# RWKV-6 attention feeding a gated MLP: the first chunk's softplus, Erf and multiplication of the sixth step take another place

## The chip, the cores and the metric

The kernel runs on one core of a Trainium2 chip. The metric is the device time of one execution in microseconds (us). The kernel before was timed three times: 603.26, 604.39 and 604.74 us, median 604.39 us.

The engines are named as in the profile: PE does matrix products (PEld loads their weights), DVE elementwise work and reductions, ACT activations and copies, POOL elementwise work too, and SP issues DMA transfers. Each engine works through its own queue of instructions in order; engines wait for each other by semaphores.

## The reference

Two blocks follow each other. The first is an attention with a decaying state, the second a projection, a gate, and a projection back:

```python
# r, k, v, w: (batch 4, heads 8, sequence 768, head_dim 48); u: (8, 48)
for t in range(S):
    cur = einsum('bhd,bhe->bhde', u * k[t], v[t])
    y[t] = einsum('bhd,bhde->bhe', r[t], state + cur)
    state = w[t][..., None] * state + einsum('bhd,bhe->bhde', k[t], v[t])

x = y as (3072 tokens, 384)
h = x @ w_in                                   # 384 -> 2048
sp = maximum(h, 0) + log1p(exp(-abs(h)))       # softplus
out = (h * erf(sp)) @ w_out                    # 2048 -> 384
```

All of it is in float32.

## The kernel before

**Steps.** The sequence is cut into 6 blocks of 128 tokens and the batch into 2 pairs, which gives 12 steps (s = 0 to 11) of 256 tokens each. In step s the attention of step s is computed while the hidden layer of step s-1 (function `hidden`, line 777: x @ w_in into a PSUM tile m, then a copy to h by ACT at line 786) and the projection back of step s-3 (function `project`, line 809, up to step 2, `project_fast`, line 885, from step 3 on) are spread between its parts. Step 5 is the sixth, and the first that runs through `attend_late`.

**The order is written by hand.** Within the scheduled region the instructions stand in each engine's queue in the order in which the Python code issues them. For the late steps a table of strings, `LATE` (with `USUAL` for the steps that have no row of their own), says what is issued at seven places of a step, named by `STAGES_LATE`: "front", "near", 0, 1, 2, 3, 4. `run_late` reads the string of the place, token by token:

- `s`: the softplus of the next chunk (line 733, ACT), into one SBUF buffer, `sp_room`, which all chunks share
- `ey`, `ep`: its Erf (line 737, ACT), from `sp_room` into a PSUM tile: y, or the lane pp1. Ahead of each softplus and each Erf ACT loads a table
- `m`: the multiplication h = h * Erf (line 742, DVE), reading the tile of the oldest Erf still open
- `P`, `H`: a piece of the projection back or of the hidden layer (PE, with ACT's copy of a finished tile)
- `F`: the next part of what is prepared for step s+1 (function `prepare`)
- `k22y`, `k11p`, `k12y`: a copy of a quarter of h into y or pp1 (line 845, ACT)
- `S1` to `S4`: sums and differences of quarters on DVE (lines 862 to 868)

A chunk is a quarter of a step's hidden layer, 128 x 1024 elements. The chunks of step 3's hidden layer are worked off in step 5.

**The places around the change, in `attend_late`.** At the start of the step come the products of a level (line 452, PE), a scaling (line 263, DVE) and a masked copy (line 464, DVE). Then follows the place "front". The first two parts of `prepare(s + 1)` follow: on POOL the running products of the decay (line 315), on DVE the near products: one product with u (line 384) and, for distances 1 to 4, the terms (line 377) and the new k (line 381). Then follows the place "near". The next part sums the terms 1 to 3 (line 367, DVE), gives POOL the terms 5 to 8, makes one product (line 398, DVE), sums the terms 0 and 4 and gives POOL the terms from 9 on; POOL's term 5 goes into the buffer that the sums read. Then DVE multiplies kT by the spread decay (line 597), the place 0 follows, then the last level's products (line 452), the spreading of blocks (line 551, copied by ACT at line 557), ACT's copies at line 471 and a scaling on DVE, then the place 1, the state products (line 538, PE), and the places 2 to 4.

**Buffers that couple the engines.** The PSUM tile y is the target of every `ey` and of `k22y` and `k12y`; an Erf into it waits until the multiplication that read its last content is done. The two PSUM tiles m of the pool `ps_m` hold the projection's outputs in step 5 until ACT has copied them (line 818); the hidden layer's pieces (line 777) then take turns in the same two tiles.

Of the kernel before, what the change touches and what calls it, by code (L numbers as in the profile page):

```python
# [17 lines left out]
P = 128  # L18
# [43 lines left out]
def kernel(  # L62
# [881 lines left out]
    def in_order(s, k):  # L944
# [3 lines left out]
        for what in order[k]:  # L948
# [8 lines left out]
    STAGES_LATE = ("front", "near", 0, 1, 2, 3, 4)  # L957
    LATE = {
        DIRECT + 1: (
            "", "", "s ey m P s ep m P P s P ey m P", "s P F ep m P k22y F P k11p F", "S1",  # L960
            "S2 S3 H k12y S4 H F", "s H ep m H H F G s H H H ep",
        ),
        n_steps - 1: (
# [57 lines left out]
    with tc.manual_schedule(  # L1021
# [72 lines left out]
        s = n_steps  # L1094
# [104 lines left out]
```

## Time and profile before

The profiled execution took 603.48 us; its span, from the first to the last instruction, is 601.5 us. Its mean granted TensorE clock is 0.997 of full speed.

| engine | busy us | share of the span |
|---|---|---|
| PE | 585.6 | 97% |
| PEld | 501.7 | 83% |
| DVE | 439.9 | 73% |
| ACT | 362.0 | 60% |
| POOL | 272.3 | 45% |

The part of the sixth step around the change, as the timeline of the trace has it:

| instruction | start us | duration us |
|---|---|---|
| ACT: first chunk's softplus (L733) | 207.97 | 1.06 |
| ACT: first chunk's Erf into y (L737) | 210.34 | 1.03 |
| DVE: last near product (L381) | 213.30 | 0.76 |
| DVE: sums of terms 1 to 3 (L367) | 213.97 | 2.37 |
| POOL: first term (L377) | 214.95 | 1.31 |
| DVE: product L398 | 216.25 | 0.95 |
| DVE: sums of terms 0 and 4 (L367) | 217.24 | 1.61 |
| DVE: product into kT (L597) | 218.77 | 1.72 |
| DVE: first chunk's multiplication (L742) | 220.41 | 1.21 |
| DVE: second chunk's multiplication (L742) | 221.54 | 1.21 |
| ACT: third chunk's Erf into y (L737) | 222.99 | 1.03 |
| DVE: third chunk's multiplication (L742) | 224.05 | 1.22 |
| ACT: fourth chunk's Erf into pp1 (L737) | 229.42 | 1.03 |
| DVE: fourth chunk's multiplication (L742) | 230.48 | 1.22 |

The table shows when each instruction began and how long it took; an engine's queue is in this order, so what stands above on the same engine is done first. Consecutive instructions on DVE overlap by some 0.1 us in the records.

### The profile page before, as it was taken

The page shows a single profiled execution, that of the slowest core. Times are in us where ns is not written, and L with a number is a line of the kernel's source. Part 1 is how long each engine was busy: PE and PEld are TensorE (multiplying, and loading weights), DVE is VectorE, ACT ScalarE, POOL GpSimd, SP SyncE. Part 2 cuts the span into 40 slices and gives each one's busy share as a digit, 9 for nine tenths or more (in the row PEclk, how much of TensorE's full clock was granted, in tenths as well). Part 3 has the DMA queues.
Part 4 walks back from the last instruction along what each step waited for, and adds up shares of the span by engine and source line. Part 5 has one row for each costly group of instructions (what it writes and reads, how often), then busy time and mean ns, then how long its engine had stood idle before and what let it go on. Part 6 is the DMA issues. An engine that isn't in the chain of part 4 may idle for free.

```text
span 601.5 us, 16645 instructions
## 1 busy us (share of the span) xinstructions
PE 585.6 (97%) x7290; PEld 501.7 (83%) x7290; DVE 439.9 (73%) x516; ACT 362.0 (60%) x473; POOL 272.3 (45%) x296
## 2 busy tenths in 40 slices
PE   7889999999999997999999999999999999999997
PEld 6668787578668756899899899898898898898997
DVE  5688598798996898699799799799799624124140
ACT  2548888726534477684865864765765764756710
POOL 4349275601487569429639639539549100000000
PEclk9999999999999998999999999999999999999999
DMA  8377371541314415234334324334321300000000
GB/s 323 116 278 231 131 273 61 212 142 20 140 50 155 93 48 192 46 105 169 71 105 168 71 105 169 72 106 133 71 106 54 71 9 26 2 21 13 2 27 26
DMA packets 51376, 63.33 MB, mean 105 GB/s; under 512 B 34920, under 2 KB 40296, under 8 KB 49896
## 3 DMA queue, kind: packets, MB, share of 16 engines
q1 hardware_dynamic: 50824, 62.03, 31.9%
q8 instruction: 57, 0.93, 0.6%
q10 hardware_dynamic: 480, 0.25, 0.2%
q14 instruction: 15, 0.12, 0.1%
HBM read 52.39 MB, written 8.69 MB: 102 GB/s over the span
## 4 chain that ended last, share of the span: by engine, by line
PE 81%; DVE 8%; DMA 4%; ACT 3%; issue 2%; POOL 2%; SPq 0%; POOLq 0%; DVEq 0%; ACTq 0%
PE m L777 38%; PE m L885 28%; PE m L809 4%; PE pp L452 4%; DMA w<-in_rkw 3%; PE y L486 2%; PE y L512 1%; DVE in L263 1%; PE pp L538 1%; DVE sums L367 1%; DVE words L381 1%; DVE rk L377 1%; POOL tot_sb L315 1%; POOL w_in_sb L232 1%; DVE own L464 1%
## 5 line engine op out<-in xcount | busy, mean ns | idle before, releaser
L777 PE MATMUL m<-xT,w_in_sb 128*128 128x256 f32 x1152 | 259.3, 383 | 5.7 <-ACT o L818 3.2
L777 PEld LDWEIGHTS m<-xT,w_in_sb 128*128 128x128 f32 x1152 | 217.2, 191 | 38.9 <-issue 3.8
L786 ACT COPY h<-m 128x512 f32<-128x512 f32 x96 | 55.8, 582 | 85.8 <-PE m L777 85.7
L263 DVE TENSOR_TENSOR in<-in,tot_sb 128x1024 f32<-128x1024 f32 (+1 forms) x60 | 78.7, 1311 | 24.6 <-PE pp L452 21.6
L377 POOL TENSOR_TENSOR rk<-words 128x528 f32<-128x528 f32 (+3 forms) x28 | 40.7, 1455 | 98.5 <-DVE sums L367 88.1
L381 POOL TENSOR_TENSOR words<-words,rest 128x528 f32<-128x528 f32 (+10 forms) x77 | 79.5, 1033 | 6.0
L809 PE MATMUL m<-w_out_sb,h 128*128 128x384 f32 x192 | 64.3, 491 | 0.0
L809 PEld LDWEIGHTS m<-w_out_sb,h 128*128 128x128 f32 x192 | 35.7, 190 | 23.6
L885 PE MATMUL m<-mixed,h 128*128 128x192 f32 x288 | 51.1, 331 | 0.0
L885 PE MATMUL m<-w_out_sb,h 128*128 128x192 f32 x288 | 50.3, 329 | 0.0
L737 ACT ACT_TABLE_LOAD x36 | 46.2, 1283 | 4.9 <-DVE h L742 3.2
L733 ACT ACT_TABLE_LOAD x36 | 46.2, 1283 | 2.6 <-issue 2.0
L885 PEld LDWEIGHTS m<-w_out_sb,h 128*128 128x128 f32 x288 | 46.9, 190 | 0.5
L885 PEld LDWEIGHTS m<-mixed,h 128*128 128x128 f32 x288 | 46.6, 190 | 0.9
L452 PEld LDWEIGHTS pp<-in 48*64 48x64 f32 (+1 forms) x2368 | 33.8, 125 | 14.4 <-issue 7.7
L885 PE MATMUL m<-w_out_sb,room 128*128 128x192 f32 x256 | 44.2, 326 | 0.0
L315 POOL TENSOR_TENSOR tot_sb<-tot_sb 128x256 f32<-128x256 f32 (+4 forms) x60 | 40.4, 673 | 4.5
L742 DVE TENSOR_TENSOR h<-h,y 128x1024 f32<-128x1024 f32 x17 | 20.7, 1215 | 29.6 <-ACT y L737 29.5
L885 PEld LDWEIGHTS m<-w_out_sb,room 128*128 128x128 f32 x256 | 42.0, 190 | 0.0
L452 PE MATMUL pp<-in 48*64 48x64 f32 (+1 forms) x2368 | 38.4, 212 | 3.8 <-issue 1.6
L733 ACT ACTIVATE room<-h 128x1024 f32<-128x1024 f32 x36 | 38.1, 1057 | 0.4
L742 DVE TENSOR_TENSOR h<-h,pp 128x1024 f32<-128x1024 f32 x19 | 23.0, 1212 | 20.8 <-ACT pp L737 20.8
(123 smaller groups left out, 822.1 us busy)
## 6 DMA issues: line engine op xcount, KB each, us to landing
in<-in_rkw SPq DMA_DIRECT2D x11, 1024.0 KB, 5.6
words<-in_moe_w_in SPq DMA_DIRECT2D x8, 768.0 KB, 6.2
words<-in_moe_w_out SPq DMA_DIRECT2D x8, 768.0 KB, 4.6
words<-in_rk_rows SPq DMA_DIRECT2D x8, 768.0 KB, 6.0
w<-in_rkw SPq DMA_DIRECT2D x11, 512.0 KB, 6.9
v<-in_v SPq DMA_DIRECT2D x12, 384.0 KB, 5.6
out<-o SPq DMA_DIRECT2D x24, 192.0 KB, 2.5
rest<-in_w_rows SPq DMA_DIRECT2D x8, 384.0 KB, 5.3
```

The source lines that it names most:

```text
L263: nc.vector.tensor_mul(halves, halves, view(tots[level - 1], 0, [[1, n], [2, nb], [0, half]]))
L315: nc.gpsimd.tensor_mul(new, pair[:, :, 0], pair[:, :, 1])
L377: engine.tensor_mul(terms[n], r[:, :, n:], k[:, :, : near - n])
L381: engine.tensor_mul(k[:, :, :m], k[:, :, :m], w[:, :, n : n + m])
L452: nc.tensor.matmul(pp[s0 : s0 + m, e, n, :m], lhsT=rk[rows(e), 1, n, s0 : s0 + m], rhs=rk[rows(e), 0, n, t0 : t0 + m], start=True, stop=True,)
L733: nc.scalar.activation(sp_room, chunks[0], AF.Softplus)
L737: nc.scalar.activation(at, sp_room, AF.Erf)
L742: nc.vector.tensor_mul(h, h, at)
L777: nc.tensor.matmul(ps[:, ff, :], lhsT=w_in_sb[:, g * FG + f + ff, kk * P : (kk + 1) * P], rhs=xT[:, kk, :], start=kk == 0, stop=kk == KT - 1,)
L786: nc.scalar.copy(h[:, f : f + FT, :], ps[:])
L809: nc.tensor.matmul(ps[j][:], lhsT=gs[g][:, f, j * C : (j + 1) * C], rhs=w_out_sb[:, g * FG + f, :], start=g + f == 0, stop=g == NG - 1 and ...
L885: nc.tensor.matmul(to, lhsT=a[:, f], rhs=b[:, f], start=start and f == 0, stop=f == FG - 1, skip_group_check=True,)
```

## The change

In the row of the sixth step the first chunk's softplus and Erf are issued at the place "front" instead of at the place 0, and its multiplication at the place "near". In the place 0 the remaining two chunks and the five pieces of the projection are strung in another order, and in the place 1 one piece of the projection is issued behind `k22y` instead of ahead of it. The number of each kind of token stays.

```diff
     STAGES_LATE = ("front", "near", 0, 1, 2, 3, 4)
     LATE = {
         DIRECT + 1: (
-            "", "", "s ey m P s ep m P P s P ey m P", "s P F ep m P k22y F P k11p F", "S1",
+            "s ey", "m", "s ep m P P s ey m P P P", "s P F ep m k22y P F P k11p F", "S1",
             "S2 S3 H k12y S4 H F", "s H ep m H H F G s H H H ep",
         ),
```

## The prediction

> **What bounds the kernel now.** I read the page's busy times first (PE 585.6 of 601.5 us, next DVE with 439.9), so only time in which PE stands still, or runs slowly, can be won. Then the waits between 204 and 254 us, which is the sixth step up to its last projection, PE's rows alone:
>
> ```profile
> engine line waited for: us in total, times, longest us
> PE m L777 <- ACT o L818: 3.2, 2, 2.2
> ```
>
> PE waits twice, each time for a copy of a finished output out of PSUM by ACT. PE's timeline from 226 us puts the two waits, and its granted clock by windows tells what followed (columns: us, length, then busy time and count for PE, PEld, DVE, ACT, POOL, then PEclk):
>
> ```profile
> 226.26 0.94 PE L538 MATMUL pp<-v,kT 64*48 64x48 f32 x64
> 228.16 2.86 PE L777 MATMUL m<-xT,w_in_sb 128*128 128x256 f32 x12 [0.97 <-ACT o L818]
> 233.22 20.08 PE L777 MATMUL m<-xT,w_in_sb 128*128 128x256 f32 x84 [2.20 <-ACT o L818]
> ```
> ```profile
> 231.10:233.20 2.10, 0.00 (x0) 0.00 (x0) 2.00 (x3) 1.46 (x3) 2.02 (x2) 1.00 0.00 0
> 233.20:236.00 2.80, 2.79 (x7) 2.26 (x8) 2.80 (x3) 1.76 (x3) 2.56 (x4) 0.53 0.63 202
> 236.00:239.00 3.00, 3.00 (x14) 2.56 (x13) 2.95 (x5) 1.84 (x3) 2.61 (x7) 0.87 1.00 382
> ```
>
> The reader is to see two losses: 0.97 + 2.20 = 3.17 us of standing still, and, right behind the second, a stretch at a granted clock of 0.53 and then 0.87. Its cost: the same 96 matmuls of the next step take 20.99 us (0.2186 each), so the 84 here should take 18.37 and took 20.08: 1.71 us more. Last, the chain of waits, followed back from that second wait:
>
> ```profile
> 220.49 1.14 DVE h L742
> ...
> 221.69 0.08 ACT L737
> 221.78 1.21 issue
> 222.99 1.03 ACT y L737
> ...
> 225.25 1.28 ACT L733
> ...
> 226.55 1.06 ACT room L733
> ...
> 227.63 0.48 ACT o L818
> ...
> 228.13 1.28 ACT L737
> ...
> 229.42 1.04 ACT pp L737
> ...
> 230.48 1.23 DVE h L742
> ```
>
> It goes on with the copy at L845 (231.74) and the second copy of an output (232.76 to 233.17), for which PE waits. Its root is the first chunk's multiplication on DVE at 220.41. The chunk's Erf had been ready on ACT since 210.34 + 1.03 = 211.37; but the multiplication stands behind all near products, the sums of terms 1 to 4 and the product into kT. The third chunk's Erf writes the same PSUM tile (y) and so waits for that multiplication: ACT stands still for 3.25 us (218.45 to 221.69).
>
> **What the skill says.** "TensorE: Matmul & The Clock Gate", Part 1: The HAM clock gate, states that the array falls to half of its clock after an idle window and regains it after about 3.4 us of work. The trace agrees: 0.53 of the clock after the 2.2 us gap; 1.71 us lost at half speed is 3.4 us of it. "ScalarE: Activation LUTs", What ACT_TABLE_LOAD costs: about 1283 ns for each load, whatever the set; here 1.28 us before each softplus and each Erf. "SBUF — State Buffer", Who interferes with whom: a DVE operation with two inputs in SBUF contends with GpSimd's reads. The trace agrees: the same L263 of 512 elements takes 1.43 us in this step and 0.68 in the next. The multiplication of this change has one input in PSUM.
>
> **The change part by part.** The instructions that each engine issues, and their order on PE, ACT, POOL and SP (its DMAs among them), stay as they were: nothing on these engines stands between the places from which and to which the first softplus, its Erf and one piece of the projection move. Only DVE's order changes: the first chunk's multiplication (h<-h,y) passes seven instructions: three sums, the product L398, two sums, the product into kT L597. So there is one moved operation of 1.21 us (1.14 in sequence), nothing added or removed.
>
> Its new place: DVE ends its last near product at 213.30 + 0.76 = 214.06; the Erf is done since 211.37, so it doesn't wait (2.7 us in hand). It runs 214.0 to 215.2.
>
> Behind it on DVE, seven instructions come 1.13 us later (220.41 to 221.54 is the pitch of two such multiplications): the sums start at 215.1 instead of 213.97, the product into kT ends at about 221.6 instead of 220.49. Who waits for them: POOL, whose first term follows the first sum (214.95, now 216.1), and PE's state products L538 at 226.26, which need kT: 4.6 us in hand. Cost on the path: nothing; if that cover were gone, up to 1.13 us.
>
> What it frees on ACT: the third Erf's table load starts at 218.47 instead of 221.69, 3.22 us earlier. After it ACT has no wait of its own: PE's level products end at about 218.15 and its block spreading at 218.39, before the copies L557 and L471 (now about 220.7 to 222.0); the fourth softplus ends at 224.4; the first output (8 of its 24 rows of L809 behind 218.32, so 221.0) is copied 224.4 to 224.9; the fourth Erf ends at 227.23.
>
> DVE meanwhile: multiplications two and three at 221.54 and 222.68 (the third Erf ends at 220.8, so the old idle 1.30 goes), L263 of 512 elements (pitch 1.35) from 223.8, L263 of 1024 (1.93) from 225.17 to 227.1. The fourth multiplication starts at 227.26, 3.22 us earlier. Then L845 at 228.5, the second copy of an output ends at 229.94 instead of 233.16.
>
> PE: L538 ends at about 227.2, the first copy is done at 224.9, so L777's first 12 rows start at 227.19 (0.97 gained) and end at 229.98; the second buffer is free at 229.94. The second wait is 0 to 0.05 us: all 3.17 us go. With no gap of over 0.1 us left here I see nothing to drop the clock: another 1.71. Sum 4.88 us.
>
> What is late next: L777's further pieces need their buffer emptied by ACT. At the full clock a piece takes 12 x 0.2186 = 2.62 us. The third needs a copy that ends at about 231.4, before 232.6; the fourth one at about 234.0, before 235.25; the closest is the fifth (236.9 before 237.9). PE reaches from_own at 248.35 instead of 253.23. DVE must then have L263 of the next step ready (246.31 + 1.84 = 248.15 before). It is held by the sums of POOL's terms: POOL, 1.13 us later, gives its last products at about 239.2; the sums end at about 241 instead of 244.03, and L263 at about 245, against 248.85, when PE asks for it. The DMA of the sums goes out 3 us earlier with them. From 253 us to the end the waits list none for PE, and its work there is one row behind the other, so the gain is carried to the end.
>
> The sum against the profiled execution: its own time is 603.48 (span 601.5 and 1.98 around it); less 4.88 is 598.6. The median of the runs shown is 604.39, 0.9 above; I take 604.39 - 4.88 = 599.5.
>
> Bounds of what the trace doesn't show: the clock's fall may still come elsewhere (0 to 1.71 us kept; I take 0, because the only gap left is under 0.1 us). The moved DVE work meets other POOL work: between the sums and the fourth multiplication are the product into kT (1.72 us, with 0.95 as an undisturbed size of 768 elements), and L263 at 1.43 and 1.93. They can lose or gain some 0.7 us each, since 0.68 is seen; only 0.16 us is in hand there, so a longer one shows in PE's second wait. I take 0, bounds 0 to 1.5; a gain is excluded by ACT's Erf, which ends last.
>
> **Rivals.**
> *The waits go, the clock's spell stays or comes later:* for it speaks that two gaps preceded it and the trace doesn't tell which of them counted; against it, that with both gone nothing is left to set it off, and that the lone gap of 0.99 us ahead of 69.35 us left the clock at 1.00. 604.39 - 3.17 = 601.2.
> *The second wait stays in part*, because DVE is held by POOL in kT and L263 and the fourth multiplication comes up to 1.5 us late: 599.5 + 0.7 to 599.5 + 1.5, about 600.6.
> *Swallowed later:* POOL's terms and the sums that wait for them hold DVE until PE asks for the next level product. It decides if POOL ends about 4 us later than I reckon; with that the early time is waited off: 603.5 to 604.4. Against it: POOL's 23.5 us of terms take as long in the next step (266.44 to 290), where the multiplication already stands before the sums.
> *Slower:* the first multiplication, now ahead of the sums, stands waiting for its Erf, and everything behind it on DVE (the sums, POOL's 22 operations, kT, the fourth multiplication) stands too. ACT's start there hangs on its three DMA issues (to 206.64). The path is late from 0.16 us of stall on and the gain is gone at 4.9 us, if the Erf ended at 218.9 instead of 211.37; with 7 us, 604.39 + 2.1 = 606.5. Since ACT's order didn't change, I see no reason for this delay.
>
> **How the numbers follow.** Chances: forecast (599.5, own range 598.3 to 600.3) 0.62; spell stays (601.2) 0.13; second wait in part (600.6) 0.11; swallowed 0.08; slower 0.06. The range 598.2 to 602.0 holds the first three but for a little. A measurement of this kernel tells about 0.3%, 1.8 us, from no change: all of the first three (0.86) are faster than 602.6; same 0.08; slower 0.06.
>
> **What would show it.** Right: on DVE h<-h,y directly before the three sums without idle time; ACT's wait of 3.2 us for DVE gone; PE's waits for o L818 gone; L777's 96 rows in about 21 us and a clock of 1.00 between 226 and 250 us. Wrong: DVE idle before that multiplication, a clock under 1 in this stage, a wait of PE for L263, or a DVE still busy with POOL's sums when from_own has begun.

## The result, and the profile after

The changed kernel took 598.26 us in the median of 6 executions (597.87 to 599.63), beside it the kernel before 603.83 us (601.60 to 605.25, 6 executions). The ratio is 0.9913 with a 95% interval of 0.989 to 0.9936. In a later comparison it was 598.21 us against 603.25 us, 0.9929 (0.9905 to 0.9953). The profiled execution took 598.50 us, its span is 596.3 us (before 601.5).

PE's timeline in the sixth step, as in the prediction (start, duration, instruction; idle time ahead of it would stand in brackets):

```profile
226.26 0.94 PE L538 MATMUL pp<-v,kT 64*48 64x48 f32 x64
227.12 21.01 PE L777 MATMUL m<-xT,w_in_sb 128*128 128x256 f32 x96
248.06 0.66 PE L486 MATMUL y<-own,v 64*48 64x64 f32 x32
```

L538 starts at the same 226.26 us as before. Behind it all 96 rows of L777 (records: each of these 48 float32 matmuls has two) run in one piece, without the waits of 0.97 and 2.20 us, and the products of the function `from_own` (L486), which come next, start at 248.06 instead of 253.23. The stage from L538 to from_own has shrunk from 26.97 to 21.80 us, by 5.17; the span by 5.2. From from_own to the end it is some 348.2 us in both. So the whole difference lies in this stage, and nothing of it is given back.

The windows of the changed kernel over that stretch (columns as in the prediction; the last but two is the granted clock):

```profile
228.20:231.00 2.80, 2.80 (x15) 2.36 (x14) 2.70 (x3) 2.74 (x4) 2.64 (x3) 1.00 0.18 60
231.00:234.00 3.00, 3.00 (x16) 2.64 (x15) 2.95 (x5) 1.57 (x3) 2.76 (x4) 1.00 0.91 311
234.00:237.00 3.00, 3.00 (x16) 2.64 (x15) 3.00 (x4) 2.95 (x5) 2.69 (x5) 1.00 0.70 272
```

The clock stays at 1.00 where it stood at 0.53 and 0.87. DVE's timeline of the changed kernel shows the moved instruction and what it pushes:

```profile
213.97 1.22 DVE L742 TENSOR_TENSOR h<-h,y 128x1024 f32<-128x1024 f32 x1
215.10 2.37 DVE L367 TENSOR_REDUCE sums<-rk 128x15 f32<-128x720 f32 x3
...
219.90 1.72 DVE L597 TENSOR_TENSOR kT<-kT,spread 128x768 f32<-128x768 f32 x1
221.54 1.21 DVE L742 TENSOR_TENSOR h<-h,pp 128x1024 f32<-128x1024 f32 x1
222.67 1.21 DVE L742 TENSOR_TENSOR h<-h,y 128x1024 f32<-128x1024 f32 x1
223.80 0.68 DVE L263 TENSOR_TENSOR in<-in,tot_sb 128x512 f32<-128x512 f32 x1
224.40 2.12 DVE L263 TENSOR_TENSOR in<-in,w 128x1024 f32<-128x1024 f32 x1
227.00 1.22 DVE L742 TENSOR_TENSOR h<-h,pp 128x1024 f32<-128x1024 f32 x1 [0.48 <-ACT pp L737]
...
243.21 1.68 DVE L263 TENSOR_TENSOR in<-in,tot_sb 128x1024 f32<-128x1024 f32 x1
```

The first multiplication has no idle time ahead of it, the product into kT is 1.13 us later, the fourth multiplication 3.48 us earlier, and the scaling for the next step's products (243.21 + 1.68 = 244.89) is 3.7 us ahead of PE's L452 at 248.55. ACT's timeline has the link between them. First the table load ahead of the third Erf in the kernel before, then ACT in the changed kernel:

```profile
221.69 1.28 ACT L737 ACT_TABLE_LOAD   x1 [3.25 <-DVE h L742]
```
```profile
217.14 1.06 ACT L733 ACTIVATE room<-h 128x1024 f32<-128x1024 f32 x1
218.21 1.28 ACT L737 ACT_TABLE_LOAD   x1
219.51 1.03 ACT L737 ACTIVATE y<-room 128x1024 f32<-128x1024 f32 x1
...
224.15 0.48 ACT L818 COPY o<-m 128x384 f32<-128x384 f32 x1
...
229.21 0.47 ACT L818 COPY o<-m 128x384 f32<-128x384 f32 x1
```

The third Erf's table load follows the softplus at once, where ACT waited 3.25 us before. The copies of the two outputs, for which PE used to wait, end at 224.63 and 229.68 instead of 228.11 and 233.16.

### The profile page after: what moved, and what is told of

It is laid out like the page before. It is cut to its first block, busy times and chain, and to the rows that moved or that the text cites. A ratio compares the mean times of both kernels' runs of the same rounds, so it can differ in the third digit from the quotient of the medians.

```text
span 596.3 us, 16645 instructions
## 1 busy us (share of the span) xinstructions
PE 584.7 (98%) x7290; PEld 501.7 (84%) x7290; DVE 440.1 (74%) x516; ACT 361.8 (61%) x473; POOL 274.5 (46%) x296
## 4 chain that ended last, share of the span: by engine, by line
PE 88%; DVE 6%; issue 2%; ACT 2%; DMA 1%; POOL 1%; SPq 0%; DVEq 0%; ACTq 0%; POOLq 0%
PE m L777 40%; PE m L885 28%; PE m L809 8%; PE pp L452 6%; PE y L486 2%; DVE in L263 2%; PE pp L538 1%; PE y L512 1%; DMA in<-in_rkw 1%; PE pp L680 1%; DVE sums L367 1%; DVE words L381 1%; DVE own L464 1%; ACT rk L292 1%; DVE w_in_sb L228 0%
## 5 line engine op out<-in xcount | busy, mean ns | idle before, releaser
L777 PE MATMUL m<-xT,w_in_sb 128*128 128x256 f32 x1152 | 257.3, 382 | 2.3 <-DVE w_in_sb L228 1.3
L777 PEld LDWEIGHTS m<-xT,w_in_sb 128*128 128x128 f32 x1152 | 216.0, 190 | 34.5 <-issue 3.7
L263 DVE TENSOR_TENSOR in<-in,tot_sb 128x1024 f32<-128x1024 f32 (+1 forms) x60 | 78.3, 1305 | 24.9 <-PE pp L452 23.8
L377 POOL TENSOR_TENSOR rk<-words 128x528 f32<-128x528 f32 (+3 forms) x28 | 41.6, 1485 | 91.4 <-DVE sums L367 81.0
L381 POOL TENSOR_TENSOR words<-words,rest 128x528 f32<-128x528 f32 (+10 forms) x77 | 79.1, 1027 | 6.0
L809 PE MATMUL m<-w_out_sb,h 128*128 128x384 f32 x192 | 64.3, 491 | 0.0
L809 PEld LDWEIGHTS m<-w_out_sb,h 128*128 128x128 f32 x192 | 35.7, 190 | 23.6
L452 PEld LDWEIGHTS pp<-in 48*64 48x64 f32 (+1 forms) x2368 | 34.0, 125 | 14.8 <-issue 8.1
L452 PE MATMUL pp<-in 48*64 48x64 f32 (+1 forms) x2368 | 38.7, 212 | 4.0 <-issue 1.8
```

Of the source, the lines that this page charges most:

```text
L263: nc.vector.tensor_mul(halves, halves, view(tots[level - 1], 0, [[1, n], [2, nb], [0, half]]))
L377: engine.tensor_mul(terms[n], r[:, :, n:], k[:, :, : near - n])
L381: engine.tensor_mul(k[:, :, :m], k[:, :, :m], w[:, :, n : n + m])
L452: nc.tensor.matmul(pp[s0 : s0 + m, e, n, :m], lhsT=rk[rows(e), 1, n, s0 : s0 + m], rhs=rk[rows(e), 0, n, t0 : t0 + m], start=True, stop=True,)
L777: nc.tensor.matmul(ps[:, ff, :], lhsT=w_in_sb[:, g * FG + f + ff, kk * P : (kk + 1) * P], rhs=xT[:, kk, :], start=kk == 0, stop=kk == KT - 1,)
L809: nc.tensor.matmul(ps[j][:], lhsT=gs[g][:, f, j * C : (j + 1) * C], rhs=w_out_sb[:, g * FG + f, :], start=g + f == 0, stop=g == NG - 1 and ...
```

## The experiments

Each kernel ran beside executions of the kernel before on the same chip. The stage is the time from L538's start to from_own's start in the profiled execution; in experiment 5, where L538 itself waits 0.50 us, that wait is counted in.

| kernel | median us (before beside it) | ratio and 95% interval | stage us |
|---|---|---|---|
| before | | | 26.97 |
| changed | 598.26 (603.83) | 0.9913 (0.989 to 0.9936) | 21.80 |
| changed, again | 598.21 (603.25) | 0.9929 (0.9905 to 0.9953) | 21.81 |
| 1: multiplication back | 603.19 (603.15) | 1.0001 (0.9988 to 1.0014) | 26.97 |
| 2: Erf into SBUF | 599.65 (603.15) | 0.9946 (0.9927 to 0.9964) | 22.36 |
| 3: both gaps filled | 601.78 (603.15) | 0.999 (0.9979 to 1.0001) | 25.29 |
| 4: multiplication ahead of kT | 599.96 (603.15) | 0.9955 (0.9938 to 0.9971) | 23.65 |
| 5: multiplication at front | 604.72 (603.18) | 1.0027 (1.0012 to 1.0043) | 27.64 |
| 6: first gap filled | 603.52 (603.18) | 1.001 (0.9996 to 1.0023) | 26.97 |
| 7: second gap filled | 602.04 (603.18) | 0.9984 (0.9974 to 0.9994) | 25.31 |
| 8: multiplication amid the sums | 598.66 (603.25) | 0.9931 (0.9907 to 0.9954) | 21.78 |

**1: is it the multiplication alone?**

```diff
-            "s ey", "m", "s ep m P P s ey m P P P", ...
+            "s ey", "", "m s ep m P P s ey m P P P", ...
```

> Only the multiplication goes back to the place 0; the first softplus and Erf stay at the place front, the pieces of the projection in the changed order. Theory (only DVE's order matters, the other tokens change no engine's queue): as before, within 1 us of it; PE's two waits for o L818 are back with 3.2 us. Rival (the earlier place of the softplus and Erf, or of the piece behind k22y, does part of the work): part of the gain stays, 1 to 4 us below before.

PE's timeline of this kernel:

```profile
225.92 0.94 PE L538 MATMUL pp<-v,kT 64*48 64x48 f32 x64
227.82 2.86 PE L777 MATMUL m<-xT,w_in_sb 128*128 128x256 f32 x12 [0.97 <-ACT o L818]
232.87 20.08 PE L777 MATMUL m<-xT,w_in_sb 128*128 128x256 f32 x84 [2.19 <-ACT o L818]
```

It is the stage of before to 0.01 us. The other tokens of the change do nothing.

**2: the tile y, or DVE's order?** The order of before; the first chunk's Erf goes to a free quarter of `room`.

```diff
+        if kind == "r":
+            return room[:, 1]
...
-            "", "", "s ey m P s ep m P P s P ey m P", ...
+            "", "", "s er m P s ep m P P s P ey m P", ...
```

> DVE's order as before, the multiplication behind kT; but the first chunk's Erf is written into a free SBUF buffer instead of y, so that the third Erf has nothing to wait for. Theory (the gain comes through the tile y: ACT no longer waits for DVE): 4.8 to 5.3 us below before, ACT's 3.2 us wait for the multiplication and PE's waits for o L818 gone. Rival (DVE's order itself is what counts, through the sums, POOL or the fourth multiplication): no change, within 1 us of before.

DVE's, POOL's, ACT's and PE's timelines of this kernel, in this order:

```profile
218.16 1.73 DVE L597 TENSOR_TENSOR kT<-kT,spread 128x768 f32<-128x768 f32 x1
219.80 2.22 DVE L744 TENSOR_TENSOR h<-h,room 128x1024 f32<-128x1024 f32 x1
```
```profile
219.14 1.80 POOL L381 TENSOR_TENSOR words<-words,rest 128x480 f32<-128x480 f32 x1
221.02 1.96 POOL L377 TENSOR_TENSOR rk<-words 128x432 f32<-128x432 f32 x1
```
```profile
216.41 1.06 ACT L735 ACTIVATE room<-h 128x1024 f32<-128x1024 f32 x1
217.49 1.28 ACT L739 ACT_TABLE_LOAD   x1
```
```profile
225.64 0.94 PE L538 MATMUL pp<-v,kT 64*48 64x48 f32 x64
226.51 21.56 PE L779 MATMUL m<-xT,w_in_sb 128*128 128x256 f32 x96
```

The multiplication stands behind kT as before. But the third Erf's table load follows the third softplus at once (217.49 behind 217.47), and PE's two waits are gone all the same: the gain comes through the tile y and ACT, not through DVE's order. The rival falls. The gain is 0.56 us smaller in the stage than the change's (22.36 against 21.80): the multiplication now reads two inputs in SBUF beside POOL's terms and takes 2.22 us instead of 1.21. That agrees with "SBUF — State Buffer", Who interferes with whom, in the Trainium skill. Two inputs in SBUF are not slow by themselves: L263 of 1024 elements, which has them too, takes 1.22 us at 204.43 us of the kernel before, where POOL stands idle. The delay goes on down the chain: ACT's first copy at L847 waits 1.75 us for DVE instead of 1.29, and PE's weight loads (PEld) wait 0.5 and 0.3 us for emptied buffers, against 0.2 in the changed kernel. The median fell short of what I expected, 3.5 us below before instead of 4.8 to 5.3. It is 1.4 us above the changed kernel's, of which the stage explains 0.56; the rest is open (the profiled execution, 598.47 us, was the fastest of the six).

**3: what the clock cost.** Extra matmuls fill the gaps; the waits stay. So that nine of them can stand behind the first piece of L777, that piece (`H`) is issued in the place 2 instead of the place 3.

```diff
         state_part(s, kT, ps)
+        idle[:] = [ps[1][:, :, D:]]
+        if s == DIRECT + 1:
+            fill(4)
         run(2, following)
...
-            "s P F ep m P k22y F P k11p F", "S1",
-            "S2 S3 H k12y S4 H F", ...
+            "s P F ep m P k22y F P k11p F", "S1 H D",
+            "S2 S3 k12y S4 H F", ...
+    def fill(n):
+        for _ in range(n):
+            nc.tensor.matmul(
+                idle[0], lhsT=w_in_sb[:, 0, :P], rhs=w_in_sb[:, 0, P : 2 * P], start=True, stop=True,
+                skip_group_check=True,
+            )
...
+            elif what == "D":
+                fill(9)
```

> The order of before, with 13 extra matmuls of 128 columns into columns of a PSUM tile that nobody reads: 4 behind L538, 9 behind the first piece of L777, that fill PE's two gaps (each matmul some 0.22 us, so 0.9 and 2.0 us) without ending them earlier. Theory (the gaps made the clock fall, and that costs 1.71 us beside the 3.17 of the waits): 1.4 to 2.0 us below before, granted clock 1.00 from 233 to 239 us, the 84 rows of L777 in about 18.4 us. Rival (the clock fell for another reason, or the slow rows cost nothing on the path): no change, within 0.5 us, or a bit slower.

PE's timeline (each extra matmul has two records), and a window of the stretch that stood at 0.53 and then 0.87 before:

```profile
227.01 1.16 PE L979 MATMUL pp<-w_in_sb 128*128 128x128 f32 x8
228.06 2.86 PE L780 MATMUL m<-xT,w_in_sb 128*128 128x256 f32 x12
230.75 2.17 PE L979 MATMUL pp<-w_in_sb 128*128 128x128 f32 x18
233.11 18.40 PE L780 MATMUL m<-xT,w_in_sb 128*128 128x256 f32 x84 [0.19 <-ACT o L821]
```
```profile
234.00:237.00 3.00, 3.00 (x16) 2.64 (x15) 2.96 (x5) 1.95 (x3) 2.69 (x5) 1.00 0.98 312
```

The second piece of L777 starts 6.96 us behind L538, as in the kernel before, so the waits are untouched. The 84 rows take 18.40 us instead of 20.08: 1.68 us, as reckoned, and the stage shrinks by just that. In the profile the theory holds. The medians are 1.4 us apart, but the interval of the ratio reaches 1. The reason is in the executions of before: the mean granted clock was below 0.9985 in 20 of 36 (median 603.49 us) and at or above it in 16 (median 601.63). Here it was below in 4 of 21, and the other 17 have a median of 601.74. So filling the gaps brings nothing to an execution that kept its clock (601.74 against 601.63); it only makes the others rarer.

**4: is every microsecond passed on?**

```diff
-            "s ey", "m", "s ep m P P s ey m P P P", ...
+            "s ey", "", "s ep m P P s ey m P P P", ...
...
+        if s == DIRECT + 1:
+            run_late(s, "m")
         kT = kTs[s]
```

> The multiplication stands behind the sums, directly ahead of the product into kT: one instruction of 1.64 us earlier than before instead of seven. Theory (what ACT gains is passed on one to one): the third Erf comes 1.64 us earlier, PE's first gap goes, one of about 1.6 us stays behind the first piece of L777; the waits shrink by 1.64 us. If such a gap alone leaves the clock at 1.00, 3.3 us below before; if the clock falls as before, 1.6 us below. Rival (any place ahead of kT gives the whole gain): 5 us below.

ACT's and PE's timelines and a window of this kernel:

```profile
219.77 1.28 ACT L739 ACT_TABLE_LOAD   x1 [1.87 <-DVE h L744]
```
```profile
226.84 2.86 PE L779 MATMUL m<-xT,w_in_sb 128*128 128x256 f32 x12
231.29 18.40 PE L779 MATMUL m<-xT,w_in_sb 128*128 128x256 f32 x84 [1.60 <-ACT o L820]
```
```profile
231.00:234.00 3.00, 2.71 (x13) 2.40 (x14) 2.90 (x4) 1.70 (x4) 2.84 (x3) 1.00 0.61 135
```

ACT still waits 1.87 us for the multiplication. The first gap of PE is gone, 1.60 us of the second is left, and the clock stays at 1.00 behind it; over the whole execution its mean was 0.999 or 1.000 in all 7. The median is 3.2 us below before, the stage 3.32 us shorter: 1.6 of waits and 1.7 of clock. Against the executions of before that kept their clock (601.63) it is 1.7 us, the waits alone. The rival falls.

**5: the slower rival, brought about.**

```diff
-            "s ey", "m", "s ep m P P s ey m P P P", ...
+            "s ey m", "", "s ep m P P s ey m P P P", ...
```

> The multiplication stands still further ahead, at the place front, before the near products, where its Erf isn't ready: this is the slower rival of the prediction, brought about. Theory (DVE stands for 4.8 us until the Erf ends at about 211.1; everything behind it comes about 6 us later, less 1.1 us that leave its old place; the third Erf is early, but the fourth multiplication comes at about 231.6 and the second output copy ends at about 234.3): one gap of PE of some 4 us ahead of the second piece of L777, from L538's start to from_own 26.3 us with the clock at 1.00 or 28.0 with a spell, against 26.97 before; the time is 4.5 to 6.2 us above the changed kernel, 0 to 2 us above before. Rival (any place ahead of the sums gives the gain, since PE has 4.6 us in hand for kT): 5 us below before.

DVE's and PE's timeline, and a window:

```profile
211.09 1.22 DVE L742 TENSOR_TENSOR h<-h,y 128x1024 f32<-128x1024 f32 x1 [4.79 <-ACT y L737]
...
224.71 1.72 DVE L597 TENSOR_TENSOR kT<-kT,spread 128x768 f32<-128x768 f32 x1
```
```profile
226.74 0.94 PE L538 MATMUL pp<-v,kT 64*48 64x48 f32 x64 [0.50 <-PE m L809]
227.60 2.86 PE L777 MATMUL m<-xT,w_in_sb 128*128 128x256 f32 x12
233.99 19.96 PE L777 MATMUL m<-xT,w_in_sb 128*128 128x256 f32 x84 [3.53 <-ACT o L818]
```
```profile
234.00:237.00 3.00, 3.00 (x7) 2.46 (x8) 2.90 (x3) 1.36 (x2) 2.87 (x2) 0.50 0.67 184
```

DVE stands for 4.79 us. The product into kT ends at 226.43, and PE's state products, which need it, wait 0.5 us (the profile puts this wait down to PE itself, whose rows of L809 had ended at 226.24). One gap of 3.53 us follows, and the clock falls. The time is 1.5 us above before, and 6.5 above the change, a little more than the 4.5 to 6.2 that I expected. So the mechanism is real; the change stays clear of it because the near products cover the time until the Erf is there.

**6 and 7: which of the gaps drops the clock?** Experiment 3 with one of its two fillings left out. In 6 the string of place 2 is "S1" and that of place 3 is as before; in 7 the four matmuls behind the state products are left out.

```diff
-            "s P F ep m P k22y F P k11p F", "S1 H D",
-            "S2 S3 k12y S4 H F", ...
+            "s P F ep m P k22y F P k11p F", "S1",
+            "S2 S3 H k12y S4 H F", ...
```

> The order of before with only the first gap of PE filled (4 extra matmuls), the second one of 2.2 us stays. Theory (the two gaps count together: a lone gap of 1.6 us left the clock at 1.00 in all 7 executions of the kernel with the multiplication ahead of kT): the clock stays at 1.00 in most executions, the median some 1.5 us below before, its fastest executions as fast as those of before. Rival (the 2.2 us gap alone makes the clock fall): 0.997 in about half of the executions as in before, no change of the median.

> The order of before with only the second gap of PE filled (9 extra matmuls), the first one of 0.97 us stays. Both theories: the clock stays at 1.00 in most executions, the median some 1.5 us below before, the fastest executions as those of before; if half of them still show 0.997, the spell doesn't come from the long gap.

PE's timeline of the kernel with the first gap filled, then of the one with the second filled:

```profile
233.06 20.08 PE L780 MATMUL m<-xT,w_in_sb 128*128 128x256 f32 x84 [2.20 <-ACT o L821]
```
```profile
234.23 18.40 PE L778 MATMUL m<-xT,w_in_sb 128*128 128x256 f32 x84 [0.19 <-ACT o L819]
```

With the first gap filled, the 84 rows still take 20.08 us, and the clock was below 0.9985 in 17 of 21 executions. My theory that the two gaps count together falls: the gap of 2.2 us does it alone. With that one filled, the profiled execution has the rows at 18.40 us and the median is 1.1 us below before; 8 of its 21 executions were still below 0.9985. For the profiled one of these the trace says where: its granted clock is 0.94 in the first 30 us and 1.00 in this stage. For the others it isn't known. So a mean clock below 0.9985 says that the clock fell in an execution, but not where.

**8: how late may it be?** The multiplication goes between the sums of terms 1 to 3 and the product L398.

```diff
             sum_up(1, 2, 3)
+            if s == DIRECT + 2:
+                yield
             term(nc.gpsimd, 5, 6, 7, 8)
...
         next(following, None)
+        if s == DIRECT + 1:
+            run_late(s, "m")
+            next(following, None)
...
-            "s ey", "m", "s ep m P P s ey m P P P", ...
+            "s ey", "", "s ep m P P s ey m P P P", ...
```

> The multiplication stands between the sums of terms 1 to 3 and the product L398, 2.3 us later than in the changed kernel, and POOL's first term 1.1 us earlier. Theory (what counts is only that the multiplication is done when ACT is through with the third softplus, about 218.4; here it ends at about 217.4): ACT and PE as in the changed kernel, from L538's start to from_own 21.8 us, the time within 0.5 us of the changed kernel's. Rival (every microsecond that the multiplication comes later is paid, as between the place ahead of kT and the place before): 2.3 us above the changed kernel.

> The changed kernel once more, for its median and the granted clock of its executions beside more executions of before. Theory: 598.3 us, the clock at 0.997 or below in few executions (in 1 of 6 so far), since no gap of PE is left in the stage; before 603.2 with the clock below 0.9985 in more than half.

DVE's, ACT's and PE's timelines of experiment 8:

```profile
217.04 1.21 DVE L747 TENSOR_TENSOR h<-h,y 128x1024 f32<-128x1024 f32 x1
```
```profile
217.78 1.06 ACT L738 ACTIVATE room<-h 128x1024 f32<-128x1024 f32 x1
218.86 1.28 ACT L742 ACT_TABLE_LOAD   x1
```
```profile
227.90 20.99 PE L782 MATMUL m<-xT,w_in_sb 128*128 128x256 f32 x96
```

The multiplication ends at 218.25, before ACT is through with the third softplus (218.84 in this execution), and the stage is 21.78 us, the change's. What counts is that one deadline, not an early place. In experiment 4 the multiplication ended at 219.69, 1.78 us behind the third softplus (217.91), and that was paid. In the repeat of the changed kernel the clock was below 0.9985 in 2 of 8 executions, beside 8 of 13 of before. No kernel of the study is faster than the changed one.

## Why the prediction was right

The forecast was 599.5 us, a gain of 4.88 us on the profiled execution; 598.26 us and 5.0 us (603.48 to 598.50) were measured. The sum from the profiled execution, 598.6 us, was close; the 1.2 us between 599.5 and 598.26 are nearly all in the base. 604.39 was the median of three executions, and the 93 of the same kernel in the later comparisons have a median of 603.2. So the measured median lies just under the narrow range of the forecast (598.3 to 600.3), though the mechanism held.

- *The chain of waits and its root.* Right: experiment 1 shows that the multiplication is all of it, experiment 2 that it acts by holding the tile y, experiment 8 that its deadline is the end of the third softplus.
- *The seven instructions pushed back cost nothing.* Right: the product into kT ends at 221.62 (221.6 reckoned), and PE's L538 starts at 226.26 as before. Experiment 5 shows the price once that cover is used up.
- *ACT 3.22 us earlier, the fourth multiplication at 227.26.* It started at 227.00: ACT began its first table load 0.24 us earlier in this execution (206.43, not 206.67). DVE had 0.48 us in hand and not 0.16, because the L263 of 512 elements took 0.68 us and not 1.43, against 2.12 instead of 1.93 for the next one. The prediction had read 1.43 us in this step against 0.68 in the next as the price of POOL's work; but POOL works beside the shorter one too (L263 at 273.04, POOL's L377 at 273.13). The records differ in which of the two began first. Before, L263 began at 225.19, behind POOL's L381 (225.07), and L263 took longer. In the changed kernel it began at 223.80, ahead of POOL's L381 (223.94), and L381 took longer, 1.50 us instead of 1.10. That it fell this way was not foreseen. The rival in which POOL makes this late did not come.
- *3.17 us of waits.* Right in sign and place, a little small: a gap also lays bare the end of the rows ahead of it, which overlaps with the next rows where these follow at once. The 12 rows alone took 2.86 us, where 12 x 0.2186 is 2.62, and L538 overlaps with L777 by 0.08 us in the changed kernel. These 0.24 and 0.08 us go with the gaps: 3.49 us. With 1.68 us of clock that is 5.17 us, what the stage lost.
- *1.71 us of clock.* The size is right (1.68 in experiment 3, by the profile), and so is the cause, a gap of PE. The term was mis-sized in one respect: I took it as paid in each execution. In the three comparisons after the first, the clock of before was below 0.9985 in 57 of 93 executions. Those have a median of about 603.5 us, the others of about 601.6. Against the change's 598.2 the first lose 5.3 us, the others 3.4, which is the waits alone. Not each of the 57 need have lost its clock in this stage: the kernels that leave no gap there, or 0.97 us at most, are below 0.9985 too in 18 of 68 executions. The medians compare as forecast only because more than half of before's are of the first kind; that is luck, for the prediction looked at one execution.
- *The rival with the spell kept.* It was argued against with a lone gap of 0.99 us that left the clock at 1.00. Experiment 4 supports that for 1.6 us; experiment 6 shows that it doesn't hold for 2.2.
- *The slower rival.* Rightly held unlikely, but priced too low: the gain was to be gone at a stall of 4.9 us. In experiment 5 such a stall, of 4.79 us, took the gain and 1.5 us more, since the price left out that the longer gap makes the clock fall (1.56 us: 19.96 against 18.40) and that the state products come late (0.50 us).
- *Nothing given back later.* Right: POOL's last product ends at 239.24 (239.2 reckoned), the scaling for the next step at 244.89 (245), and PE waits for nothing from 248 us to the end.

## What to carry to other kernels

When an engine that is far from full (ACT here, 60%) ends PE's wait, follow the chain back past it: the cause may be a reader that stands in another engine's queue behind work that isn't urgent and holds a buffer. Such a reader needs to be early enough for one deadline; ahead of that it gains nothing, and put before its own input is there it stalls the whole queue. Count a gap of PE with the clock that it may cost, but as a chance and not as a certainty, and look at the granted clock of many executions before its share is named.

## What the runs showed of the hardware

- With a gap of PE of 1.6 us in this stage the mean clock was below 0.9985 in 0 of 7 executions, with one of 2.2 us in 17 of 21, with one of 3.5 us in 7 of 8. Kernels without a gap in this stage, or with 0.97 us at most, had it below in 4 of 21 (experiment 3), 8 of 21 (7), 3 of 14 (changed), 1 of 6 (2) and 2 of 6 (8), from elsewhere: in the profiled executions of 7 and 8 the clock fell between 16 and 21 us. The prediction had drawn on "TensorE: Matmul & The Clock Gate", Part 1: The HAM clock gate, where the fall is put after an idle window of about 3.4 us; here a gap of 2.2 us was enough in most executions, and the measurement decides.
- The length of a fall did not depend on the gap. In six profiled executions the clock fell while PE still had work to come (before, 1, 5, 6 in this stage, 7 and 8 near their start), and in all six it stood at 0.50 for 3.41 us, by windows of 0.1 us. In this stage the fall began between 0.2 us before PE's rows went on (experiment 5) and 1.3 us after (experiment 1, whose windows follow; the rows had gone on at 232.87):

```profile
233.00:234.00 1.00, 1.00 (x5) 0.90 (x6) 1.00 (x1) 1.00 (x2) 0.92 (x2) 1.00 0.30 106
234.00:235.00 1.00, 1.00 (x5) 0.80 (x4) 1.00 (x2) 0.26 (x1) 0.92 (x2) 0.57 1.15 195
235.00:236.00 1.00, 1.00 (x4) 0.82 (x3) 0.99 (x3) 0.70 (x1) 0.84 (x3) 0.50 0.80 319
236.00:237.00 1.00, 1.00 (x4) 0.73 (x4) 0.97 (x2) 0.31 (x1) 0.84 (x3) 0.50 0.96 363
237.00:238.00 1.00, 1.00 (x5) 0.86 (x4) 1.00 (x2) 0.78 (x2) 0.84 (x3) 0.72 1.03 407
```

- What the windows lack to full clock is 0.43 + 0.50 + 0.50 + 0.28 = 1.71 us, the price of a fall where PE has work throughout (20.08 against 18.40 us for the 84 rows). In experiment 5 part of it lay in the gap, and the rows took 19.96 us. Over a span of 601 us, 1.71 us are 0.0028: a mean clock of 0.997 stands for about one such fall, and 0.9985 parts the executions with one from those without.
- The multiplication of 1024 elements takes 1.21 us with one input in PSUM and took 2.22 us with both in SBUF while POOL was working. In that trace (experiment 2) POOL's L381, begun earlier, ended at 220.94 us, and the multiplication 1.08 us later, at 222.02: as if it had waited for L381 to end.
